# A fused attention, MoE and soft-MoE kernel: F in 512-column matmuls over plain 32x32 transposed tiles, w_out turned in the last pass, b = 7 in program order

## The chip, the cores and the metric

The kernel runs on one core of a Trainium2 chip. The metric is the device time of one execution in microseconds (us). The kernel before takes 537.74 us, the median of three runs (536.98 to 540.11). On this kernel a difference of about 0.5% (2.7 us) is what a measurement can tell from none.

## The reference

An attention between 512 tokens and 32 state rows of each of 8 batches and 8 heads, in both directions, gives 8 x 544 = 4352 rows of 512. These pass a gated two-layer projection and then a soft mixture of experts with 32 slots. Cut to what is computed:

```python
# x (8, 8, 512, 64), state (8, 8, 32, 64)
s = x @ state.T / 8;  xread = softmax(s) @ state        # tokens read the state
s2 = state @ x.T / 8; sread = softmax(s2) @ x           # the state reads tokens
x = concatenate([xread, sread], axis=2)                 # -> (4352, 512)
h = x @ w_in                                            # (512, 2048)
g = where(h >= 1, h, where(h <= -1, 0, (h + 1) ** 2 / 4))
y = g @ w_out                                           # (2048, 512)
logits = y @ phi                                        # 32 slots = 8 experts x 4
d = softmax(logits, over rows);  slot_in = d.T @ y
slot_out = relu(slot_in @ w1[e]) @ w2[e]                # w1 (512, 1024), w2 (1024, 512)
out = softmax(logits, over slots) @ slot_out
```

## The kernel before

y is never formed. With wp = w_out phi the logits are g wp (the matmuls `E`, in `estep`), and slot_in = (d.T g) w_out. So the kernel keeps a running sum over batches of d.T g (`acc`, 32 slots x 2048, laid out over 128 partitions) with a running maximum, and turns it into slot_in once at the end (`SI`).

**Passes.** There is one pass per batch, b = 0 to 7, over its 512 token rows, and a ninth (b = B = 8) over the 256 state rows of all batches (`XS`). A pass has 16 steps m of 128 columns of w_in: `hstep` makes h (12 matmuls of 128x512, each fp32 product from two rounded halves) and g from it (one ScalarE, one GpSimd and one VectorE operation). g lies with its columns on partitions and tokens along the row. Between the steps lie the attention of the next batch (`attention`), the chunks of its x (`vchunk`, matmuls `V`), and, one batch late, the weighting of g.

**F.** d.T g needs g with tokens on partitions. `tstep` turns every 32x32 block of a finished g tile with VectorE and scatters the blocks into one of three places of 4096 columns (`gp0` to `gp2`, each half a batch; `gd_of`) in the order that lets `fall` read 256 columns in a row. `smblock(b)` is a generator of steps that makes the softmax weights (`dRp`, `dR`) and calls `fall`: 128 matmuls of 32x32 weights by 256 columns, in 8 rounds of 16 (half h, row block r), each round filling the 4x4 grid of 32x32 parts of the array (t over array columns, k over array rows); three VectorE operations then fold F into `acc`. Batch 0 goes another way: TensorE turns its g tiles (`tquarter`, tile `gtp`), ScalarE copies them out to `wb`, and four groups of 128x32 matmuls (`F<-wb,dN`, L600 on) and four copies (L605) start `acc`. The ninth pass turns its g the same way into `gp1`, and weights it by the matmuls `P`.

**Weights.** w_in and w_out come as packed words and are converted during batch 0 (`conv_win`, `conv_wo`). For w_out the words go to `acc` one quarter at a time, TensorE turns them (`wtp`, 64 transposes), ScalarE copies them to `wD`, and a DMA writes the turned w_out to DRAM (`wo32`), from where `prefetch` brings it back; `wps`, 4 matmuls for each 2 quarters, makes wp. The end needs 4 MB of w_out, 16 MB of w1 and 16 MB of w2. Their loads are issued in a fixed sequence, one each time a place in SBUF comes free (`give`): six on GpSimd's queue, the others on SyncE's (SP). A load on a queue waits until its place has been read for the last time, and those behind it wait too.

**End.** After the ninth pass: `P`, its transposes `PTp` (L894), `SI` (L901, 16 matmuls of 128x32 by 512), `XDp`, the first expert layer (`h`, L920), `hTp` (L941), and for each half of the 512 columns `SO(0)` and `SO(1)` (L954: w2_0 to w2_7, w2_8 to w2_15), `SR`, the combination of the rows `oV`, `oX`, `oH`, and 16 stores of 512 KB (L993).

**What sets the order.** A list scheduler orders every engine's instructions by readiness and priority, except TensorE's in b = 2 to 6, where the function `steady` runs under a manual schedule and TensorE follows the code. b = 0, 1, 7 and the ninth pass are written in the general loop and ordered by the scheduler on all engines.

Of the kernel before, what the change touches and what calls it, by code (L numbers as in the profile page):

```python
# [16 lines left out]
CFG = dict(wb=12, gv6=(5, 9, 12), lP=((0, 0), (0, 1)), attA=(3, 5, 6, 7, 8, 9, 10, 11), attB=(0, 1, 10, 11, 12), attN=(14, 15), dv=(9, 12, 14), fl=-0.484375, hp=2000, att7=(3, 5, 6, 7, 8, 10), og=1, n3=1, n3m=10, wS=['DP', 'AD', 'AD', 'AD', 'AD', 'DP', 'AD', 'DD', 'AD', 'AD', 'AD', 'AD', 'AD', 'AD', 'AD', 'AD'], xsm=13, k0=5, rg=6, spg=0, att0=6, att=7, V0=(2, 6, 10), Vn=(0, 4, 10), Vx=12, wn='H', wsev='adad', conv=(4, 8, 9, 11, 12, 13, 19, 21, 24, 26, 28, 32, 36, 40, 44, 48, 52, 56, 60), todo=[1, 1, 1, 2, 0, 0, 0, 3, 0, 0, 2, 2, 1, 1, 0, 0], E0=2, E=1, sm=1, tqB=(5, 9, 13), GP=10, pe=(3,), psH=3, gtpX=(0, 7), tq0=(13, 15), keep=(2, 3, 4, 5), x2=(1, 1), natm=1, warm=14, bounce7=(0, 3), split=1, wt=4, so='cscscscscssss', smm=(1, 2, 3, 4, 5, 6, 9), tqv=(), tqvm=0, first='x', apath=2, f32c=1, place=1, attm=(3, 6, 7, 8, 9, 12), subPm=True, loDm=False, bounce=(0, 1, 2, 3), bq=('s', 's'), xq='s', nat=((1, 11), (2, 2), (2, 3), (2, 11), (3, 2), (3, 4), (3, 9), (4, 2), (4, 3), (4, 9), (5, 2), (5, 3), (5, 9), (6, 2), (6, 4), (6, 9)), subP=(1,), mulD=(), loD=(), qlag=0, gv0='EEEEEEEEEEEEEEEE', gv='EEEEEEEEEEEEEEEE', gvS='BBBBBBBBBBBBBBBB')  # L17
# [3 lines left out]
def kernel(  # L21
# [56 lines left out]
    dN = const.tile([128, 4, 32], F32, name="dN")  # L78
# [5 lines left out]
    gp_s = [slot(f"gp{c}", n=4096) for c in range(3)]  # L84
    g0_s = [gp_s[c // 2][:, 2048 * (c % 2):2048 * (c % 2) + 2048] for c in range(6)]
# [48 lines left out]
    cw_w = [acc[:, 512 * i:512 * i + 512] for i in range(4)]  # L134
# [89 lines left out]
    def attention(b):  # L224
# [15 lines left out]

        def over_tokens():
            for G in range(2):
                mx = small.tile([128, 1], F32, tag=f"mx{G}", name="mx")
                nc.vector.tensor_reduce(out=mx, in_=S[G], op=ALU.max, axis=AX.X)
                nb = small.tile([128, 1], F32, tag=f"nb{G}", name="nb")
# [801 lines left out]
```

## Time and profile before

| | |
|---|---|
| median of three runs | 537.74 us |
| runs | 540.11, 536.98, 537.74 us |
| the profiled execution | 533.0 us |
| its span in the profile | 531.0 us (2.0 us lie outside) |
| granted TensorE clock, mean | 0.972 of full |
| first g of b = 0, 1, 2, 3, 4, 5, 6, 7, ninth pass | 33.3, 103.6, 153.7, 201.8, 245.5, 290.0, 334.0, 375.1, 418.7 us |

The rows further down are of this execution. Busy time is counted for each engine by itself, matmuls of different parts of the array run side by side, and "idle before" names the time an engine stood before a group and what released it. The passes b = 2 to 6 take about 44 us each and look alike, so one block, 187 to 231 us, stands for them.

### The profile page before, as it was taken

How to read it: one execution, taken by the hardware profiler on the slowest of the kernel's cores; microseconds unless marked ns; L12 is line 12 of the kernel's file. 1: busy time of each engine (PE TensorE's matmuls, PEld its weight loads, DVE VectorE, ACT ScalarE, POOL GpSimd, SP SyncE). 2: the span in 40 equal slices, each digit the busy share in tenths (PEclk: the TensorE clock that was granted, in tenths of full speed). 3: DMA queues.
4: the chain of work that ended last, by engine and by line, in shares of the span. 5: the costliest groups of instructions: out<-in, count | busy, mean ns of one | idle time of the engine just before them, and what ended most of it. 6: DMA issues, size and time to landing. Idle time of an engine off the chain costs nothing.

```text
span 531.0 us, 12486 instructions
## 1 busy us (share of the span) xinstructions
PE 460.5 (87%) x5262; PEld 276.1 (52%) x5262; DVE 365.1 (69%) x638; ACT 271.9 (51%) x497; POOL 226.4 (43%) x221
## 2 busy tenths in 40 slices
PE   5478697999989999998999999999986989789981
PEld 3135354665546555565655655555653768534550
DVE  2888959566688689689679878967857748315240
ACT  2899767655565365267347536525514436411241
POOL 2443434444465195377348529537515400002220
PEclk9799989999999999999999999999999999999996
DMA  8997727700260130030022013004201679799999
GB/s 312 417 422 330 197 120 160 234 4 3 80 238 1 26 136 0 5 133 27 4 80 80 1 22 141 0 4 153 85 4 41 218 268 386 279 372 423 411 358 299
DMA packets 22551, 85.92 MB, mean 162 GB/s; under 512 B 2017, under 2 KB 10593, under 8 KB 14305
## 3 DMA queue, kind: packets, MB, share of 16 engines
q1 hardware_dynamic: 20976, 77.28, 39.8%
q0 software_dynamic: 1520, 7.87, 4.4%
q8 instruction: 41, 0.67, 0.5%
q14 instruction: 14, 0.11, 0.1%
HBM read 72.03 MB, written 13.11 MB: 160 GB/s over the span
## 4 chain that ended last, share of the span: by engine, by line
PE 42%; DVE 24%; issue 11%; ACT 10%; POOL 6%; DMA 4%; SPq 0%; ACTq 0%; POOLq 0%; DVEq 0%
PE h L437 14%; DVE g L489 5%; DVE gp L512 4%; POOL c L467 4%; PE h L445 3%; PE E L118 3%; PE SO L954 3%; DMA gp<-in_win_dram 3%; PE h L920 3%; POOL a L320 2%; DVE v L387 2%; ACT c L129 2%; PE V L118 2%; PE gtp L507 2%; DVE acc L172 2%
## 5 line engine op out<-in xcount | busy, mean ns | idle before, releaser
L437 PE MATMUL h<-a,v 128*128 128x512 f32 x744 | 196.5, 408 | 12.9 <-DVE g L489 7.3
L467 POOL TENSOR_TENSOR c<-c 128x512 f32<-128x512 f32 x128 | 137.3, 1081 | 149.9 <-ACT c L129 149.3
L437 PEld LDWEIGHTS h<-a,v 128*128 128x128 f32 x744 | 133.6, 189 | 78.6 <-issue 26.6
L129 ACT ACTIVATE c<-h,half 128x512 f32<-128x512 f32 x128 | 86.9, 691 | 96.8 <-PE h L437 46.9
L489 DVE SCALAR_TENSOR_TENSOR g<-h,c 128x512 f32<-128x512 f32 x112 | 75.4, 674 | 38.7 <-POOL c L467 38.5
L512 DVE STREAM_TRANSPOSE gp<-g 128x512 f32<-128x512 f32 x112 | 78.8, 704 | 2.5
L129 ACT ACTIVATE v<-V 128x512 fp32r<-128x512 f32 x62 | 37.2, 600 | 35.8 <-DVE v L387 27.5
L124 PE MATMUL FX<-gp,dR 32*32 32x256 f32 x896 | 38.6, 385 | 2.3 <-issue 2.3
L387 DVE TENSOR_TENSOR v<-V,v 128x512 fp32r<-128x512 f32 x52 | 35.0, 673 | 7.9 <-ACT v L129 7.4
L124 PE MATMUL FV<-gp,dR 32*32 32x256 f32 x882 | 38.2, 385 | 1.3 <-issue 1.3
L124 PE MATMUL V<-win,st_t 64*32 64x512 f32 x448 | 37.0, 623 | 0.0
L118 PE MATMUL V<-win,st_t 64*32 64x512 f32 x64 | 34.7, 623 | 2.3 <-ACT att L129 2.3
L118 PE MATMUL E<-g,wp 128*32 128x512 f32 x56 | 30.0, 619 | 4.6 <-DVE g L489 4.4
L288 POOL TENSOR_TENSOR att<-att,z 128x512 f32<-128x512 f32 x16 | 17.3, 1083 | 31.2 <-DVE rz L252 16.0
L124 PE MATMUL E<-g,wp 128*32 128x512 f32 x168 | 30.4, 619 | 0.0
L445 PE MATMUL h<-XSh,v 128*128 128x256 f32 x128 | 25.0, 288 | 0.9 <-DVE s_gc L493 0.5
L619 DVE SCALAR_TENSOR_TENSOR acc<-acc,al,FV 128x1024 f32<-128x1024 f32 x7 | 9.0, 1281 | 23.4 <-PE FX L124 20.4
L124 PEld LDWEIGHTS FX<-gp,dR 32*32 32x32 f32 x896 | 20.7, 103 | 7.5 <-issue 4.6
L124 PEld LDWEIGHTS FV<-gp,dR 32*32 32x32 f32 x882 | 21.3, 103 | 5.9 <-issue 2.3
L320 POOL TENSOR_TENSOR a<-att,a 128x512 fp32r<-128x512 f32 x14 | 17.8, 1290 | 11.9 <-ACT a L129 11.8
L445 PEld LDWEIGHTS h<-XSh,v 128*128 128x128 f32 x128 | 20.2, 188 | 3.1 <-ACT v L129 0.8
L266 POOL TENSOR_TENSOR att<-att,m 128x512 f32<-128x512 f32 x14 | 15.0, 1081 | 9.4 <-DVE m L265 7.8
(244 smaller groups left out, 765.3 us busy)
## 6 DMA issues: line engine op xcount, KB each, us to landing
w<-in_w_dram SPq DMA_DIRECT2D x23, 1024.0 KB, 9.8
xn<-in_xn_dram SPq DMA_DIRECT2D x8, 1024.0 KB, 6.2
out_dram<-o SPq DMA_DIRECT2D x16, 512.0 KB, 6.7
xs<-in_xs_dram SPq DMA_DIRECT2D x7, 1024.0 KB, 5.0
w<-in_w_dram POOLq DMA_DIRECT2D x6, 1024.0 KB, 5.5
gp<-in_wout_dram SPq DMA_DIRECT2D x5, 1024.0 KB, 11.1
wb<-in_win_dram SPq DMA_DIRECT2D x4, 1024.0 KB, 12.4
wo<-wD SPq DMA_DIRECT2D x16, 256.0 KB, 4.4
```

The source lines that it names most:

```text
L118: first = mm(**calls[0])
L124: e = mm(**c)
L129: return nc.scalar.activation(out=out, in_=in_, func=func, **kw)
L288: (nc.vector if b in CFG["mulD"] else nc.gpsimd).tensor_tensor(out=t3, in0=t3, in1=z1.unsqueeze(2).to_broadcast([128, 16, 32]), op=ALU.mult)
L320: (nc.vector if b in CFG["loD"] or b > 1 and CFG["loDm"] else nc.gpsimd).tensor_tensor(out=lo[:, G, :], in0=raw[G], in1=hi[:, G, :], op=AL ...
L387: nc.vector.tensor_tensor(out=lo[:, G, :], in0=V[G], in1=hi[:, G, :], op=ALU.subtract)
L437: mm(out=h, lhsT=v[:, G, f], rhs=a[:, G, :], start=(k == 0), stop=(k == 5))
L445: mm(out=h, lhsT=w[:, j, :], rhs=x[:, j, :], start=(k == 0), stop=(k == 11))
L467: nc.gpsimd.tensor_tensor(out=c, in0=c, in1=c, op=ALU.mult)
L489: gI[b, m] = nc.vector.scalar_tensor_tensor(out=g, in0=h, scalar=1.0, in1=c, op0=ALU.max, op1=ALU.min)
L512: nc.vector.transpose(out=gd_of(b, m // 8)[:, :, :, m % 8, :].rearrange("p c a i -> p a c i"), in_=gT[b, m].rearrange("p (a c i) -> p a c ...
L920: mm(out=h1[hf][32 * kt:32 * kt + 32, :], lhsT=XD[e // 4][:, kt, 32 * (e % 4):32 * (e % 4) + 32], rhs=w[kt], start=(e == 0), stop=(e == 7))
```

## The change

1. **F.** The three places of 4096 columns become one of 12288, which holds 24 tiles of 512 columns. `tstep` is a plain VectorE transpose of one 128x512 tile into tile ((2b + m // 8) mod 3) x 8 + m mod 8. `fall` reads it with a strided operand (runs of 32 columns, a step of 512 columns from run to run) in 64 matmuls of 32x32 by 512: 4 rounds of 16. `acc` changes its column order, and F is folded in by four VectorE operations of 512 (eight of 256 for b = 1, 4 and 7, whose tiles wrap around the place).
2. **b = 0 by the same way.** `tquarter` is kept for the ninth pass alone; batch 0 gets 16 VectorE transposes in place, four each at (b, m) = (0,11), (0,14), (1,0), (1,2); its E groups stand at (0,10), (0,13), (0,15), (1,1), its `smblock` steps from b = 1, m = 3, and `fall(0)` copies F into `acc`.
3. **w_out.** The words go straight to `wD`, and from there unturned to `wo32`; the 64 transposes and 16 ScalarE copies at the start go. `wturn`, at m = 7 to 14 of the ninth pass, turns the prefetched w_out in place: 8 transposes into one two-bank tile of `psV`, one ScalarE and one VectorE copy, eight times. `SI` has 64 matmuls of 128 columns for its 16 of 512.
4. **b = 7** runs in `steady` too, without attention, with `xsplit` and the first `wsplit` at m = 13.
5. **Places.** All weight loads go to SP's queue. `wb0` and `wb1` are given at b = 1, m = 0 (before: m = 12), `a0` at the start of b = 7. The ninth pass's turned g lies in the two places of `rot_g`, which are given only after `smblock(B)`; the 12288 columns are given in `merge`, behind `fall(7)`, and take w2_10 to w2_15 in six loads in a row (`ends`).

```diff
-    gp_s = [slot(f"gp{c}", n=4096) for c in range(3)]
+    gp = slot("gp", n=12288)
...
+    def gd_of(b, m):
+        n = ((2 * b + m // 8) % 3) * 8 + m % 8
+        return gp[:, 512 * n:512 * n + 512]
...
-        words(i, acc[:, 1024 * h:1024 * h + 1024])
+        words(i, wD[g][:, 2 * h:2 * h + 2, :].rearrange("p k f -> p (k f)"))
         for k in range(2 * h, 2 * h + 2):
-            w = cw_w[k]
-            tp = psX.tile([128, 4, 128], F32, tag="X", name="wtp")
-            for x in range(4):
-                nc.tensor.transpose(tp[:, x, :], w[:, 128 * x:128 * x + 128], ident)
-            act(wD[g][:, :, 128 * k:128 * k + 128], tp)
+            dma(out=wo32[k][:, 512 * g:512 * g + 512], in_=wD[g][:, k])
...
     def tstep(b, m):
-        nc.vector.transpose(
-            out=gd_of(b, m // 8)[:, :, :, m % 8, :].rearrange("p c a i -> p a c i"),
-            in_=gT[b, m].rearrange("p (a c i) -> p a c i", a=4, i=32))
+        nc.vector.transpose(out=gd_of(b, m), in_=gT[b, m])
...
-        for k in range(4):
-            if k >= len(CFG["tq0"]):
-                tquarter(b, k)
-            F = psX.tile([128, 512], F32, tag="X", name="F")
-            group([dict(out=F[32 * t:32 * t + 32, :], lhsT=dN[:, t, :], rhs=nat_of(b, k)[:, t], start=True, stop=True) for t in range(T)])
-            nc.vector.tensor_copy(out=acc_t[:, :, 4 * k:4 * k + 4, :], in_=F.rearrange("p (m k i) -> p k m i", m=4, k=4))
-            yield
...
-        group([dict(out=F[k][32 * t:32 * t + 32, 256 * h:256 * h + 256], lhsT=dR[32 * k:32 * k + 32, r, 32 * t:32 * t + 32],
-                    rhs=gd_of(b, h)[32 * k:32 * k + 32, r, t].rearrange("p m i -> p (m i)"), start=(r == 0), stop=(r == 3))
-               for h in range(2) for r in range(4) for t in range(4) for k in range(4)], chain=True)
-        for a, f in ((acc[:, 0:1024].rearrange("p (k f) -> p k f", k=2), V), (acc[:, 1024:1536], X[0]), (acc[:, 1536:2048], X[1])):
-            nc.vector.scalar_tensor_tensor(out=a, in0=a, scalar=al, in1=f, op0=ALU.mult, op1=ALU.add)
+        u = 2 * b % 3
+        if u < 2:
+            g = gp[:, 4096 * u:4096 * u + 8192].rearrange("p (m t r i) -> p t r m i", t=4, r=4, i=32)
+            halves = [(slice(0, 16), slice(0, 16))]
+        else:
+            g = gp.rearrange("p (u m t r i) -> p t r u m i", u=3, t=4, r=4, i=32)[:, :, :, 0::2]
+            halves = [(slice(0, 8), slice(8, 16)), (slice(8, 16), slice(0, 8))]
+        group([dict(out=F[k][32 * t:32 * t + 32, :], lhsT=dR[32 * k:32 * k + 32, r, 32 * t:32 * t + 32],
+                    rhs=g[32 * k:32 * k + 32, t, r], start=(r == 0), stop=(r == 3))
+               for r in range(4) for t in range(4) for k in range(4)], chain=True)
...
+    def ends():
+        t = slot("ends", tag="gp", n=12288)
+        for j in range(6):
+            i = len(slices) - 6 + j
+            load(i, [t], 2048 * j)
...
+    def wturn(n):
+        k, g = divmod(2 * n, 4)
+        tp = psV.tile([128, 2, 512], F32, tag="V", name="wtp")
+        for j in range(2):
+            w = where["wo", k][1][g + j]
+            for x in range(4):
+                nc.tensor.transpose(tp[:, j, 128 * x:128 * x + 128], w[:, 128 * x:128 * x + 128], ident)
...
-        if 2 <= b <= 6:
+        if 2 <= b < B:
...
-    give("gp1")
+    give([(rot_g, "g", 2048)], [(rot_g, "g", 2048)])
...
-    for i in range(4):
-        for jj in range(4):
-            mm(out=SI[32 * jj:32 * jj + 32, :], lhsT=PT[:, jj, 32 * i:32 * i + 32],
-               rhs=where["wo", i][1][jj], start=(i == 0), stop=(i == 3))
+    group([dict(out=SI[32 * x:32 * x + 32, 128 * k:128 * k + 128], lhsT=PT[:, x, 32 * g:32 * g + 32],
+                rhs=where["wo", k][1][g][:, 128 * x:128 * x + 128], start=(g == 0), stop=(g == 3))
+           for k in range(4) for g in range(4) for x in range(4)], chain=True)
```

The change also packs small tiles in pairs, and adds a function `fine` and some options that nothing uses.

VectorE at the end of batch 0, where the words of w_out's last quarters are made. L157 to L172 (before) and L156 to L171 (after) are these words, `gp` holds g, `v` is a chunk of x. Before:

```order
L387 TENSOR_TENSOR v_115<-V,v_115 128x512 x2
L157 TENSOR_SCALAR acc<-wb_113 128x1024
L159 SCALAR_TENSOR_TENSOR acc<-wb_113,acc 128x1024
L161 SCALAR_TENSOR_TENSOR acc<-wb_113,acc 128x1024
L489 SCALAR_TENSOR_TENSOR gp_109<-h,c 128x512
L170 TENSOR_SCALAR acc<-wb_114 128x1024
```

After:

```order
L428 TENSOR_TENSOR v_113<-V,v_113 128x512
L552 STREAM_TRANSPOSE gp<-gp 128x512 x4
L156 TENSOR_SCALAR wD<-wb_111 128x1024
L169 TENSOR_SCALAR wD<-wb_112 128x1024
L158 SCALAR_TENSOR_TENSOR wD<-wb_111,wD 128x1024
L171 SCALAR_TENSOR_TENSOR wD<-ast,wD 128x1024
L532 SCALAR_TENSOR_TENSOR gp<-h,c 128x512
```

Four transposes of batch 0's second group of g tiles have moved in ahead of the words.

TensorE at the end of b = 7, from the last matmuls of F to the first of the ninth pass (`h<-XSh`). Before:

```order
L437 MATMUL h<-a_749,v_115 128x512 x6
L118 MATMUL V<-win_106,st_t 32x512
L124 MATMUL V<-win_106,st_t 32x512 x7
L118 MATMUL E<-g,wp 32x512
L124 MATMUL E<-g,wp 32x512 x3
L437 MATMUL h<-a_749,v_390 128x512 x18
L118 MATMUL V<-win_107,st_t 32x512
L124 MATMUL V<-win_107,st_t 32x512 x7
L437 MATMUL h<-a_749,v_390 128x512 x6
L437 MATMUL h<-a_749,v_115 128x512 x12
```

After:

```order
L118 MATMUL E<-g,wp 32x512
L124 MATMUL E<-g,wp 32x512 x3
L478 MATMUL h<-a_661,v_382 128x512 x6
L118 MATMUL V<-win_107,st_t 32x512
L124 MATMUL V<-win_107,st_t 32x512 x7
L118 MATMUL E<-g,wp 32x512
L124 MATMUL E<-g,wp 32x512 x3
L478 MATMUL h<-a_661,v_382 128x512 x12
L478 MATMUL h<-a_661,v_113 128x512 x12
```

The E groups and the V chunks have changed their places among the h matmuls of the last steps, and every run of h is 6 or 12 long.

SP's queue in the ninth pass, the loads of w1 and w2 in the order of issue (a w1 or w2 of 128x512 or 128x1024 is a part of one that is spread over several places). Before:

```order
L699 DMA w1_7_4766<-in_w1_dram 128x1024
L699 DMA w1_8_4820<-in_w1_dram 128x2048
L699 DMA w1_11_4843<-in_w1_dram 128x2048 x2
L699 DMA w1_7_4767<-in_w1_dram 128x512
L699 DMA w1_9_4840<-in_w1_dram 128x2048 x2
L699 DMA w1_13_4916<-in_w1_dram 128x2048
```

After:

```order
L738 DMA w1_6_4234<-in_w1_dram 128x2048
L738 DMA ends_4159<-in_w2_dram 128x2048 x6
L738 DMA w1_5_4169<-in_w1_dram 128x512
L738 DMA w1_7_4368<-in_w1_dram 128x2048
L738 DMA w1_4_4166<-in_w1_dram 128x2048
L738 DMA w1_5_4170<-in_w1_dram 128x512
L738 DMA w1_8_4490<-in_w1_dram 128x2048
```

The six loads of `ends` now stand in the queue ahead of w1_7 and all that follow it.

## Rows read from the trace of the kernel before

**Rows 1.** The page, part 1: engine, busy us, share of the span, instructions.

```profile
PE 460.5 (87%) x5262; PEld 276.1 (52%) x5262; DVE 365.1 (69%) x638; ACT 271.9 (51%) x497; POOL 226.4 (43%) x221
```

**Rows 2.** Windows: start:end and length, busy us of each engine, clock, DMA.

```profile
core 0: us, PE busy (x) PEld busy (x) DVE busy (x) ACT busy (x) POOL busy (x), PEclk, DMA share, GB/s
60.00:93.00 33.00, 24.06 (x227) 14.19 (x226) 26.89 (x41) 21.25 (x38) 12.07 (x10) 0.88 0.57 154
93.00:148.00 55.00, 53.54 (x420) 32.81 (x420) 34.84 (x65) 31.92 (x64) 25.12 (x24) 0.98 0.26 87
187.00:231.00 44.00, 41.60 (x548) 24.66 (x548) 35.77 (x64) 22.97 (x45) 25.76 (x25) 1.00 0.14 45
375.00:419.00 44.00, 37.95 (x440) 23.66 (x432) 29.65 (x47) 17.06 (x30) 19.27 (x19) 0.96 0.16 51
434.00:464.00 30.00, 26.35 (x308) 19.86 (x287) 15.85 (x40) 14.00 (x30) 0.52 (x1) 1.00 0.89 334
472.00:488.00 16.00, 15.86 (x144) 6.45 (x144) 7.25 (x11) 2.63 (x6) 4.11 (x3) 1.00 1.01 420
```

**Rows 3.** Timeline of TensorE, a fall and E behind it: start, length, line, operation.

```profile
214.76 0.40 PE L118 MATMUL FV<-gp,dR 32*32 32x256 f32 x1
...
220.64 0.62 PE L118 MATMUL E<-g,wp 128*32 128x512 f32 x1
...
221.09 0.59 PE L118 MATMUL E<-g,wp 128*32 128x512 f32 x1
```

**Rows 4.** Windows of seven falls, instructions on FV alone: sum and mean.

```profile
sum 51.00, PE 38.26 PEld 21.36 DVE 4.78; mean PE 5.47 PEld 3.05 DVE 0.68
```

**Rows 5.** Timeline of VectorE around the same fall.

```profile
220.52 1.28 DVE L619 SCALAR_TENSOR_TENSOR acc<-acc,al,FV 128x1024 f32<-128x1024 f32 x1 [2.96 <-PE FV L124]
221.72 1.40 DVE L619 SCALAR_TENSOR_TENSOR acc<-acc,al,FX 128x512 f32<-128x512 f32 x2
```

**Rows 6.** Groups by line and form, 57 to 154 us: busy us, mean ns.

```profile
L512 DVE STREAM_TRANSPOSE gp<-g 128x512 f32<-128x512 f32 x16 | 11.3, 706 | 0.4
...
L507 PE MATMUL gtp<-cst_t,gp 128*128 128x128 f32 x64 | 9.0, 276 | 0.6 <-ACT att L129 0.4 <-ACT wb L129 0.2
...
L124 PE MATMUL F<-wb,dN 128*32 128x512 f32 x24 | 5.0, 601 | 0.0
...
L605 DVE COPY acc<-F 128x512 f32<-128x512 f32 x4 | 2.7, 677 | 1.7 <-PE F L124 1.7
```

**Rows 7.** Timeline of TensorE, 87 to 100 us.

```profile
90.32 1.06 PE L193 MATMUL wtp<-cst_t,acc 128*128 128x128 f32 x8 [2.08 <-DVE acc L161]
...
94.54 0.87 PE L193 MATMUL wtp<-cst_t,acc 128*128 128x128 f32 x4
...
98.56 0.66 PE L193 MATMUL wtp<-cst_t,acc 128*128 128x128 f32 x4
```

**Rows 8.** Timeline of TensorE, the end of b = 7.

```profile
402.08 1.66 PE L437 MATMUL h<-a,v 128*128 128x512 f32 x6 [1.21 <-DVE g L489]
...
407.96 3.06 PE L437 MATMUL h<-a,v 128*128 128x512 f32 x7 [2.47 <-DVE v L387]
```

**Rows 9.** Timeline of TensorE, the end of the kernel.

```profile
461.90 0.62 PE L118 MATMUL P<-gp,dN 128*32 128x512 f32 x1
...
462.35 0.59 PE L118 MATMUL P<-gp,dN 128*32 128x512 f32 x1
...
466.10 3.64 PE L901 MATMUL SI<-wo,tail 128*32 128x512 f32 x32 [0.75 <-ACT tail L129]
...
488.39 7.11 PE L954 MATMUL SO<-w,hTD 128*32 128x256 f32 x128 [0.52 <-ACT hTD L129]
```

**Rows 10.** Timeline of SyncE's queue: the load behind P, the stores.

```profile
463.92 0.33 SPq L699 DMA_DIRECT2D w<-in_w_dram  x1
...
500.25 24.62 SPq L993 DMA_DIRECT2D out_dram<-o  x16
```

**Rows 11.** The page, part 6: issues, KB each, us to landing.

```profile
out_dram<-o SPq DMA_DIRECT2D x16, 512.0 KB, 6.7
xs<-in_xs_dram SPq DMA_DIRECT2D x7, 1024.0 KB, 5.0
```

More of the change, by code (lines that the diff above doesn't have):

```diff
@@ L83 @@
     win_s = [slot(f"win{c}") for c in range(4)]
[L84 to L85 removed]
+    gp = slot("gp", n=12288)
+    g0_s = [gp[:, 2048 * c:2048 * c + 2048] for c in range(6)]
     xs_s = slot("xs")
@@ L258, in over_slots @@
         def over_slots():
+            m1s = two("m1", 16)
             for G in range(2):
@@ L322, in attention @@
+        if b > 99:
+            yield from fine()
+            return
         apath = b == 0 and CFG["apath"]
@@ L403, in xsplit @@
         act(h, XS)
-        nc.vector.tensor_tensor(out=l, in0=XS, in1=h, op=ALU.subtract)
+        (nc.gpsimd if CFG['xsP'] else nc.vector).tensor_tensor(out=l, in0=XS, in1=h, op=ALU.subtract)
         run["XS"] = h, l
@@ L567, in smblock @@
             run["s"] = small.tile([128, 1], F32, tag="sn", name="sn")
-            nc.vector.tensor_scalar(out=run["s"], in0=bs, scalar1=4.0, scalar2=None, op0=ALU.mult)
+            nc.vector.tensor_copy(out=run["s"], in_=bs)
         else:
@@ L718, in drain @@
             pass
+    def wturn(n):
[5 more added lines that the diff above has]
+                nc.tensor.transpose(tp[:, j, 128 * x:128 * x + 128], w[:, 128 * x:128 * x + 128], ident)
+        for j in range(2):
+            w = where["wo", k][1][g + j]
+            if CFG["wte"][j] == "A":
+                act(w, tp[:, j])
+            else:
+                nc.vector.tensor_copy(out=w, in_=tp[:, j])
     if CFG["first"] == "h":
@@ L761, in steady @@
         nx = None
-        plan = CFG["attB"]
+        plan = CFG["attB"] if A is not None else ()
+        if b == B - 1:
+            give("a0")
         for m in range(NM):
@@ L790, in steady @@
                 step(nx)
+            if b == B - 1 and m == CFG["xsm"]:
+                xsplit()
+            if b == B - 1 and m == CFG["wsm"]:
+                wsplit(0)
         drain(sm)
-        drain(A)
+        if A is not None:
+            drain(A)
         return nx
@@ L799 @@
         last = b == B
-        if 2 <= b <= 6:
-            with tc.manual_schedule(engines={mybir.EngineType.PE}):
+        if 2 <= b < B:
+            with tc.manual_schedule(engines={getattr(mybir.EngineType, e) for e in CFG['eng']}):
                 A = steady(b, A)
@@ L816 @@
                 give("a1")
-                give([(rot_g, "g", 2048)], [(rot_g, "g", 2048)])
             if last:
@@ L833 @@
                     sm = smblock(b - 1)
-            if sm is not None and (m >= CFG["sm"] if b == 1 or last or CFG["smm"] is None else m in CFG["smm"]):
+            if sm is not None and (m >= CFG["sm0"] if b == 1 else m >= CFG["sm"] if last or CFG["smm"] is None else m in CFG["smm"]):
                 step(sm)
@@ L869 @@
                     A = None
-            if last and m == 8:
-                give("gp0", "gp2")
+            if last and m in CFG["wt8"]:
+                wturn(CFG["wt8"].index(m))
             if last and m % 4 == 3:
@@ L879 @@
     estep(B, 3)
-    tquarter(B, 3)
+    tquarter(3)
     sm = smblock(B)
```

172 lines of the change are left out of this document (110 added, 62 removed).

## The prediction

> **What bounds the kernel now.** I read the page's busy shares first, then windows stage by stage, then the timelines of the stages that this change touches. On the page TensorE is busy for 460.5 of 531.0 us [rows 1]. The windows tell where that matters [rows 2]. In a block of the middle passes TensorE works 41.6 of 44 us at full clock and VectorE 35.8: what leaves TensorE there shortens the block, as long as VectorE does not grow past it. From 93 to 148 us, when batch 0's g is turned and weighted, TensorE works 53.5 of 55 us and VectorE 34.8, so TensorE bounds that stage still more plainly. From 60 to 93 us TensorE works only 24.1 of 33 and waits, among others, for the words of w_out [rows 7]: nobody's share is full, a chain of conversions sets the time. The stage of b = 7 has 6.05 us of idle TensorE in 44 and a clock of 0.96. From 472 us on the DMA engines are at share 1.01 with 420 GB/s [rows 2], and the stores end the kernel [rows 10].
>
> **F, passes 1 to 6.** A fall starts at 214.76 and the E behind it at 220.64 [rows 3], so it takes 5.88 us; the busy time of its half on FV is 5.47 on the mean of seven [rows 4]. Two passes of E over 512 columns start 0.45 us apart (220.64 and 221.09) [rows 3]; half of that, 0.225, is what 256 columns cost at the same rate. A fall is 8 rounds of 2 passes, 16 x 0.225 = 3.6 us of streaming; the other 2.28 us lie around the rounds, 0.285 each. After the change it is 4 rounds of 2 passes of 0.45, again 3.6, and 4 x 0.285 = 1.14: 4.74 us, **1.14 less**. The bounds: 0.24 less if most of the overhead goes with the column count, 2.3 less if none of it is left. I take the middle, since the weights to be loaded for a round are the same 16, and their number of rounds halves. VectorE has 2.96 us of idle time ahead of the fold [rows 5], and its fold goes from 2.68 us (1.28 and 1.40 [rows 5]) to 4 x 0.70 = 2.8 us, or for b = 4 and 7 eight halves of perhaps 0.45, 3.6. That is up to 0.9 us on an engine with 8 us to spare per block, so I cost it at nothing; were that cover gone it would be 0.9 us in two blocks. The transposes have the same size, so they stay at 706 ns [rows 6]. Six falls (b = 1 to 6) lie ahead of the ninth pass: 6 x 1.14 = **6.9 us less** (bounds 1.4 and 13.8).
>
> The Trainium skill, "TensorE: Matmul & The Clock Gate", section "Measured speedup vs the span model", puts a pack of 16 tiles at one matmul's length and 15 times about 4 ns. By it a round's overhead is an estimated 0.06 us, and halving the rounds saves 0.24 us of a fall, 1.4 of six; the sum below would come out 5.5 us later. The row speaks against it so far, with 0.285 us around each round, but no row shows what of that a longer round keeps; this is rival 2.
>
> **The start, 93 to 148 us.** What TensorE loses: the 64 transposes `gtp`, 9.0 us, and the groups `F<-wb,dN`, 5.0 us [rows 6]; the last transposes of w_out, 0.87 + 0.66 = 1.5 us [rows 7]; three of four E groups of batch 0, 3 x 0.9 = 2.7 us by two passes of 0.45 each [rows 3], which now stand before b = 1 where TensorE idles. What it gains: fall(0), 4.74 us, and four transposes for dR, 4 x 0.14 = 0.6. So 53.5 - 18.2 + 5.3 = 40.6 us. VectorE gains 8 of the 16 transposes (the others lie ahead of 93 us), 8 x 0.706 = 5.6 us, and trades four copies of 0.677 [rows 6] for the same: 34.8 + 5.6 = 40.4 us. Both are now alike. If TensorE still set the stage, at the middle block's share of 41.6 / 44, it would be 43 us, 12 less; if VectorE did, at its share there of 35.8 / 44, 50 us, 5 less. I take 46, **9 us less**, between the ends since each will sometimes wait for the other; for the range I keep 0 (rival 1) and 12. Ahead of 93 us I take no gain although the 48 transposes left there and their ScalarE copies go: in VectorE's order four of the transposes of batch 0 now stand in front of the words of w_out's last quarters, 4 x 0.706 = 2.8 us, and TensorE waits for just these words (2.08 us [rows 7]); the two about cancel, with 4 us either way.
>
> **b = 7.** Its waits are TensorE's own order: 1.21, then 2.47 us behind operations that VectorE finishes late [rows 8]. In the order of the code the h matmuls stand in runs of 6 and 12 with V and E between, as in the middle blocks. There 2.4 us idle remain in 44, here 6.05: 3.65 us less, and at full clock its 37.95 us of work shrink by 4%, 1.5 us [rows 2]. Together **5 us less** (bounds 0 and 7). The engine's order holds also for the head of the ninth pass, where nothing else is queued to fill a wait; that is in the lower bound.
>
> **The ninth pass and the end.** `wturn` adds 64 transposes on TensorE. Eight take 1.06 us [rows 7], so 8.5 us, in a stage where it is the bound: from 434 to 464 us it is busy for 26.35 of 30 [rows 2]. I take 1.6 us of it as filling idle time, and fall(7) gives 1.14 back: P comes 5.8 us later. `SI` in 64 matmuls of a quarter of the columns costs about the 3.64 us of before [rows 9]; I add 0.4. So the expert layers come 6.2 us later on TensorE alone, and SO(0), which ended at 488.39 + 7.11 = 495.5 [rows 9], would end at 501.7.
>
> The loads are later still. Before, `gp1` came free with P, at 463.92 [rows 10]. Now the places of `rot_g` come free there, at 463.9 + 5.8 = 469.7, and 13 loads of 1 MB in SP's order run from there to w2_7, the last that SO(0) needs. The first lands 5.0 us later [rows 11], the others follow at 1.05 MB / 420 GB/s = 2.5 us each [rows 2]: 469.7 + 5.0 + 12 x 2.5 = 504.7, and the last eighth of SO(0) ends 0.9 later, at 505.6, 10.1 us later than before. The chain from there to the end had a slack of about 2.5 us before, since w2_15 was the 16th load behind P (463.9 + 5.0 + 15 x 2.5 = 506.4) and SO(1) waited for it; now w2_10 to w2_15 are there early, by `ends`. So the end comes **7.5 us later**. The DMA side agrees: the last two loads land at 509.7, 3.3 us later than before, and the stores took 24.6 us from first to last issue [rows 10], so the stores alone would give 3.3. Bounds: 1 us (the turns fill idle time, places come earlier) and 12 (the six loads of `ends` also hold up w1_7 and those behind them, which the first expert layer waits for).
>
> **The sum** against the profiled execution: -6.9 - 9 - 5 + 7.5 = -13.4, 531.0 to 517.6 of span, 533.0 to 519.6 in all. The median of the runs is 4.7 above the profiled execution, so the median should go to 537.74 - 13.4 = **524.3 us**.
>
> **Rivals.**
>
> 1. VectorE becomes the bound of the start. For it: its 40.4 us against TensorE's 40.6, and the words of w_out behind the transposes. Then 93 to 148 us gains about 1.5 and not 9: 524.3 + 7.5 = 531.8.
> 2. A round's overhead goes with its columns, so that 512 columns cost nearly twice a round of 256. Falls gain 0.24 and not 1.14 each, fall(0) is 5.6: 524.3 + 5.5 + 0.9 + 0.9 = 531.6. Against it: the weights per round are the same.
> 3. Slower than before: the strided operand of `fall`, each run of 32 columns 2 KB from the next, is read at half the rate. A fall is then 8 passes of 0.9 and 1.14, 8.3 us: 2.4 more and not 1.14 less for each of the six and for fall(7), and 3.6 more for fall(0), so 7 x 3.6 + 3.6 = 28.8 above the forecast: 553. It decides once the other terms, -9 - 5 + 8.6 = -5.4, are used up: by eight falls at 0.7 more than before each, a pass of about 0.67. Against it: P reads runs of 32 with a step of 128 columns, and its passes start at 461.90 and 462.35 [rows 9], 0.45 apart as E's do; a step of 512 is not shown.
> 4. Nothing is gained in sum: the start gains 4, b = 7 gains 2, the falls 3.5, and the end loses 9.5, the transfers of w1 and w2 being what the late places delay: 537.7.
>
> **How the numbers follow.** The forecast has a chance of 0.52, with a range of its own of 516 to 531; rival 1 has 0.17, rival 2 0.13, rival 3 0.08, rival 4 0.10. 512 to 534 leaves out rival 3, most of rival 4 and a little of the forecast's low end. A measurement of this kernel can tell 0.5% (2.7 us) from no change. Faster by more (below 535.0): forecast, rivals 1 and 2, and a part of rival 4, 0.84. Within 0.5%: most of rival 4, 0.07. Slower: rival 3 and what is left, 0.09.
>
> **What would show it.** In the trace after, the fall of a middle block from its first matmul to the E behind it: 4.7 us (rival 2: 5.6; rival 3: over 8). Passes of 0.45 in it. The distance from the first g of b = 1 to that of b = 2, 50.1 us before: about 9 shorter, with TensorE's share below 0.95 there; if VectorE's is above it, rival 1. b = 7's 44 us window at clock 1.00 with some 2.4 us idle. In the end, SO(0) waiting for w2 around 500 us, P 5 to 6 us later against the ninth pass's first g, stores that start later but run without loads beside them. I am wrong if the h of the first expert layer waits for w1, if the ninth pass grows by more than 8 us, or if the middle blocks keep 44 us although the falls got shorter, VectorE then being what a block waits for.

## The result and the profile after

The changed kernel takes 514.36 us, the median of four runs (512.69 to 517.83), beside 537.82 us for the kernel before; the ratio is 0.961, with an interval of 0.953 to 0.969. Timed once more beside the last runs below it is 513.64 us (513.21 to 515.45) and 0.961 (0.957 to 0.965). The forecast was 524.3 us in a range of 512 to 534: the sign and the range held, but the gain is 23.5 us where 13.4 were forecast.

The page after, parts 1 and 4 (answers to [rows 1]), and behind them part 4 of the page before:

```profile
span 513.6 us, 10998 instructions
PE 449.2 (87%) x4497; PEld 262.5 (51%) x4497; DVE 378.6 (74%) x681; ACT 261.6 (51%) x473; POOL 221.1 (43%) x214
PE 42%; DVE 31%; DMA 10%; ACT 7%; POOL 5%; issue 2%; SPq 0%; ACTq 0%; DVEq 0%; POOLq 0%
PE 42%; DVE 24%; issue 11%; ACT 10%; POOL 6%; DMA 4%; SPq 0%; ACTq 0%; POOLq 0%; DVEq 0%
```

TensorE has 765 instructions less and 11 us less work, VectorE 13.5 us more, and the DMA engines now hold 10% of the chain that ended last, for 4%: something at the end waits for a transfer. The windows after, start:end and length, then busy us of each engine, granted clock and DMA (answers to [rows 2]; the second is the stretch of the start that the prediction spoke of, the fourth b = 7, the fifth the ninth pass, the last the wait of SO(0)):

```profile
core 0: us, PE busy (x) PEld busy (x) DVE busy (x) ACT busy (x) POOL busy (x), PEclk, DMA share, GB/s
60.00:90.00 30.00, 23.74 (x190) 12.91 (x198) 26.11 (x43) 16.24 (x29) 11.81 (x10) 0.77 0.38 133
90.00:142.00 52.00, 47.83 (x467) 25.73 (x452) 42.52 (x82) 26.44 (x52) 27.95 (x26) 1.00 0.33 122
190.00:233.00 43.00, 40.70 (x422) 23.31 (x421) 35.98 (x67) 23.20 (x45) 25.54 (x25) 1.00 0.15 50
356.00:391.00 35.00, 32.98 (x307) 19.29 (x292) 28.64 (x44) 15.74 (x29) 15.67 (x15) 1.00 0.07 24
391.00:441.00 50.00, 48.77 (x514) 39.47 (x513) 34.90 (x82) 27.85 (x59) 3.18 (x4) 1.00 0.79 307
464.00:479.00 15.00, 9.43 (x129) 4.56 (x130) 0.56 (x1) 0.77 (x2) 0.00 (x0) 0.89 1.01 415
```

Where the time went, by marks that both traces have (first g of a pass; first matmul of the ninth pass; `PTp`; the end of the span). Of each difference the part that the shorter falls explain stands beside it, measured from the first matmul of a fall to the first matmul of something else:

| stretch | before | after | difference | of it falls | forecast, with falls |
|---|---|---|---|---|---|
| start to first g of b = 3 | 201.8 | 190.0 | -11.8 | -1.8 | -10.1 |
| first g of b = 3 to that of b = 7 | 173.3 | 165.8 | -7.5 | -6.0 | -4.6 |
| b = 7, to the first `h<-XSh` | 40.5 | 34.9 | -5.6 | -1.0 | -6.1 |
| ninth pass, to `PTp` | 49.1 | 50.1 | +0.9 | -2.4 | +5.8 |
| `PTp` to the end | 66.3 | 72.8 | +6.5 | | +1.7 |
| span | 531.0 | 513.6 | -17.4 | | -13.4 |

The first g of b = 0, 1, 2 and 3 after come at 33.1, 99.8, 147.2 and 190.0 us. The two profiled executions differ by 17.4 us, the medians by 23.5; the other 6 us are taken up below, with the executions' clock.

The start up to the first g of b = 3, once more as windows: before, after, and after without batch 0's transposes (a run further down):

```profile
33.30:201.80 168.50, 148.64 (x1365) 87.96 (x1365) 128.17 (x215) 106.96 (x195) 82.35 (x74) 0.97 0.40 137
33.10:190.00 156.90, 138.22 (x1211) 75.14 (x1208) 134.78 (x236) 92.61 (x163) 81.86 (x74) 0.95 0.40 147
33.50:180.60 147.10, 135.26 (x1259) 73.06 (x1248) 123.76 (x219) 91.83 (x163) 83.21 (x74) 0.98 0.42 156
```

TensorE has 10.4 us less to do there, VectorE 6.6 us more, and TensorE stands idle for 18.7 us, where it was 19.9.

The timeline of TensorE, one fall of the middle passes after (answers to [rows 3]; start, length, line, operation):

```profile
202.94 0.61 PE L118 MATMUL FV<-gp,dR 32*32 32x512 f32 x1
203.40 0.59 PE L118 MATMUL FV<-gp,dR 32*32 32x512 f32 x1
```

The two passes of a round start 0.46 us apart, as those of E over 512 contiguous columns did: the strided operand is read at the full rate. All falls but the first take 4.39 us, 4 rounds of 0.90 and 0.20 around each. Before, that of [rows 3] took 5.88 us, 8 rounds of 0.45 and 0.285; the seven on FV and FX took 5.4 to 6.8. The fold on VectorE behind it (answers to [rows 5]):

```profile
207.41 1.41 DVE L661 SCALAR_TENSOR_TENSOR acc<-acc,al,FV 128x512 f32<-128x512 f32 x2 [1.66 <-PE FX L124]
208.74 1.40 DVE L661 SCALAR_TENSOR_TENSOR acc<-acc,al,FX 128x512 f32<-128x512 f32 x2
```

It takes 2.8 us as costed, and VectorE still waits for the fall ahead of it.

TensorE around `P`, two lines of before and then after (answers to [rows 9]):

```profile
461.31 0.27 PE L588 MATMUL dNp<-cst_t,dT 64*128 64x64 f32 x1 [0.74 <-ACT dT L129]
464.69 0.65 PE L894 MATMUL PTp<-cst_t,tail 128*128 128x128 f32 x4 [0.87 <-DVE tail L598]
...
436.01 1.09 PE L783 MATMUL wtp<-cst_t,wo 128*128 128x128 f32 x8
437.04 0.27 PE L626 MATMUL dNp<-cst_t,dT 64*128 64x64 f32 x1
...
437.91 1.92 PE L632 MATMUL P<-natS,dN 128*32 128x512 f32 x16 [0.43 <-ACT dN L129]
439.76 1.09 PE L783 MATMUL wtp<-cst_t,wo 128*128 128x128 f32 x8
440.73 0.66 PE L973 MATMUL PTp<-cst_t,tail 128*128 128x128 f32 x4
```

Two of the eight groups of w_out's turns lie where TensorE waited for ScalarE and VectorE before, 0.74 us ahead of `dNp` and 0.87 ahead of `PTp`. TensorE at the two `SR` before, then in SO(0) and at the two `SR` after:

```profile
496.06 0.70 PE L961 MATMUL SR<-tail,cst_t 128*128 128x256 f32 x2 [0.56 <-ACT tail L129]
...
510.78 0.70 PE L961 MATMUL SR<-tail,cst_t 128*128 128x256 f32 x2 [0.50 <-ACT tail L129]
...
464.49 1.93 PE L1032 MATMUL SO<-w,hTD 128*32 128x256 f32 x32 [0.52 <-ACT hTD L129]
470.07 6.14 PE L1032 MATMUL SO<-w,hTD 128*32 128x256 f32 x80 [3.65 <-DMA w<-in_w_dram]
477.08 1.07 PE L1032 MATMUL SO<-w,hTD 128*32 128x256 f32 x16 [0.86 <-DMA w<-in_w_dram]
478.71 0.70 PE L1039 MATMUL SR<-tail,cst_t 128*128 128x256 f32 x2 [0.56 <-ACT tail L129]
...
493.42 0.70 PE L1039 MATMUL SR<-tail,cst_t 128*128 128x256 f32 x2 [0.50 <-ACT tail L129]
```

SO(0) waits for w2 twice, 4.5 us in sum. From one `SR` to the other it is 14.71 us, for 14.72 before.

### The profile page after: what moved, and what is told of

It reads as the page before. It is cut to its first block, busy times and chain, and to the rows that moved or that the text cites. A ratio compares the mean times of both kernels' runs of the same rounds, so it can differ in the third digit from the quotient of the medians.

```text
span 513.6 us, 10998 instructions
## 1 busy us (share of the span) xinstructions
PE 449.2 (87%) x4497; PEld 262.5 (51%) x4497; DVE 378.6 (74%) x681; ACT 261.6 (51%) x473; POOL 221.1 (43%) x214
## 4 chain that ended last, share of the span: by engine, by line
PE 42%; DVE 31%; DMA 10%; ACT 7%; POOL 5%; issue 2%; SPq 0%; ACTq 0%; DVEq 0%; POOLq 0%
PE h L478 15%; DVE gp L552 7%; DVE g L532 6%; DMA w<-in_w_dram 6%; PE h L486 4%; PE FV L124 3%; PE E L118 3%; DMA gp<-in_win_dram 3%; POOL a L316 3%; DVE v L428 3%; PE FX L124 2%; POOL c L508 2%; PE V L118 2%; PE SO L1032 2%; PE wtp L783 1%
## 5 line engine op out<-in xcount | busy, mean ns | idle before, releaser
L478 PE MATMUL h<-a,v 128*128 128x512 f32 x744 | 200.4, 414 | 17.7 <-DVE g L532 9.0
L478 PEld LDWEIGHTS h<-a,v 128*128 128x128 f32 x744 | 135.2, 192 | 87.1 <-issue 28.2
L428 DVE TENSOR_TENSOR v<-V,v 128x512 fp32r<-128x512 f32 x52 | 34.9, 672 | 2.0 <-ACT v L129 1.3
L124 PE MATMUL FX<-gp,dR 32*32 32x512 f32 x512 | 35.7, 598 | 0.0
L124 PE MATMUL FV<-gp,dR 32*32 32x512 f32 x496 | 35.4, 597 | 0.0
L118 PE MATMUL E<-g,wp 128*32 128x512 f32 x56 | 29.2, 604 | 4.3 <-DVE g L532 4.0
L124 PE MATMUL E<-g,wp 128*32 128x512 f32 x168 | 29.6, 605 | 0.0
L1067 DVE COPY o<-oV 128x512 f32<-128x512 f32 x6 | 4.2, 692 | 25.6 <-PE oX L124 25.6
L661 DVE SCALAR_TENSOR_TENSOR acc<-acc,al,FV 128x256 f32<-128x256 f32 (+1 forms) x20 | 10.6, 584 | 14.5 <-PE FX L124 14.5
L1075 POOL DMA_DIRECT2D out_dram<-o x16 | 8.0, 507 | 30.3 <-DVE o L1067 30.3
L124 PEld LDWEIGHTS FV<-gp,dR 32*32 32x32 f32 x496 | 14.7, 103 | 9.6 <-issue 6.8
```

Source lines behind the costliest of these rows:

```text
L118: first = mm(**calls[0])
L124: e = mm(**c)
L428: nc.vector.tensor_tensor(out=lo[:, G, :], in0=V[G], in1=hi[:, G, :], op=ALU.subtract)
L478: mm(out=h, lhsT=v[:, G, f], rhs=a[:, G, :], start=(k == 0), stop=(k == 5))
L661: nc.vector.scalar_tensor_tensor(out=a, in0=a, scalar=al, in1=f, op0=ALU.mult, op1=ALU.add)
```

## The experiments

**The kernel before, again.**

> The kernel before, unchanged, once more. It is there for a second trace: the profiled execution of before took 533.0 us, 4.7 below its median, so the difference of the two traces (17.4 us of span) is 6 us short of the difference of the medians (23.5). Theory A: one execution of before differs from another by a few us at one place (a stage in which TensorE waits and the clock drops), and a second trace shows a span of 534 to 538 with one stage longer by 3 to 6 us. Rival: the second trace has the same 531 us and the same stages, and the medians are raised by something outside the span. Time: no change.

It took 536.11 us (ten runs), ratio 1.002 (0.998 to 1.007). Its trace has a span of 531.2 us and, from the first g of b = 1 on, every mark within 0.7 us of the first trace, so the traces don't show what its longer executions lose: the profiled ones, 533.0 and 533.2 us, both lie at the low end of the spread. Theory A's stage was not found. What the runs do show is the mean clock. In the last comparison below, eleven executions of before fall in two groups: 531.4 to 532.8 us at 0.968 to 0.972 (four), 535.1 to 537.7 us at 0.956 to 0.966 (seven). The order isn't strict: of the ten here, those of 532.7 and 533.2 us are at 0.961 and one of 536.0 us at 0.966.

**Rounds of the fall.** The matmuls of a fall are cut in two, on the new layout:

```diff
-    rhs=g[32 * k:32 * k + 32, t, r], start=(r == 0), stop=(r == 3))
-   for r in range(4) for t in range(4) for k in range(4)], chain=True)
+    rhs=part(h, k, t, r), start=(r == 0), stop=(r == 3))     # 256 columns
+   for h in range(2) for r in range(4) for t in range(4) for k in range(4)], chain=True)
```

> The changed kernel with the falls alone cut back: each matmul of 512 columns in two of 256, 8 rounds of 16 for 4, on the new layout with its strided operand. Theory: the rounds are what the falls gained by, so each of the eight falls goes from 4.39 back to about 5.9 us, TensorE is the bound in all of these passes, and the kernel is 8 x 1.5 = 12 us slower, about 526. Rival 1: the gain comes from elsewhere (the layout, the order of weights): falls stay at 4.4 to 4.7 us and the time at 514. Rival 2: falls are 5.9 but VectorE or GpSimd fills the blocks now, so that only half of it, 5 to 7 us, is seen.

532.26 us, ratio 0.993 (0.989 to 0.997): 18 us slower than the changed kernel. Windows of one of its falls, instructions on FV alone:

```profile
206.00:213.50 7.50, 5.84 (x128) 3.26 (x128) 0.69 (x2) 1.00 0.02 4
```

Its eight falls take 5.2 to 7.7 us, 50.3 together, where the changed kernel's take 35.2: 15.1 of the 17.2 us by which the spans differ; another 2.8 us lie between the two `SR` (17.48 us), where the clock was 0.81. So the number of rounds, with the matmuls and weight loads that double with it, is what the falls gained by, and TensorE pays for it about one to one. Rival 1 and rival 2 of this run fall. The first and the last fall are the longest with 256 columns (7.5 and 7.7 us); why those two was not tried.

**b = 7 in the general loop.** One line is undone:

```diff
-        if 2 <= b < B:
+        if 2 <= b <= 6:
```

> The changed kernel with b = 7 back in the general loop, where the scheduler orders TensorE. Theory: the order is worth what the traces show from the first g of b = 7 to the first matmul of the ninth pass, 5.6 us less of which 1.0 is the fall: 4.6 us slower, about 519. Rival: with the other parts in place the scheduler's order is as good, and less than 1.5 us is lost.

528.05 us, ratio 0.982 (0.974 to 0.989): some 11 us slower by the ratios, where 4.6 were expected. TensorE at the end of its b = 7 (timeline), and windows of b = 7 and of the stretch behind SO(0):

```profile
381.08 1.66 PE L478 MATMUL h<-a,v 128*128 128x512 f32 x6 [1.21 <-DVE g L532]
...
386.97 3.36 PE L478 MATMUL h<-a,v 128*128 128x512 f32 x7 [2.47 <-DVE v L428]
```

```profile
354.00:394.00 40.00, 34.40 (x291) 19.91 (x290) 28.20 (x44) 15.63 (x27) 16.30 (x15) 0.96 0.06 22
482.00:508.00 26.00, 24.84 (x199) 13.01 (x199) 5.67 (x9) 5.76 (x12) 4.10 (x8) 0.67 0.55 186
```

The two waits of [rows 8] are back to the digit, 1.21 and 2.47 us, and b = 7 takes 40.3 us for 34.9: 5.4 us. The start was 1.9 us quicker in this execution. The other 11.0 us of the 14.5 of span lie between the two `SR` (25.71 us for 14.71), where TensorE ran for a good part at its lower level (0.67 on the mean over 26 us), with the same instructions as the changed kernel, which kept 1.00 there. SO(0) waits 4.7 us for w2 in it and 4.5 in the changed kernel.

**The same with another order of w2.** The place of 24 tiles takes w2_0 to w2_5 in this kernel and in the next:

```diff
-            i = len(slices) - 6 + j
+            i = 20 + j
```

> b = 7 back in the general loop, and w2_0 to w2_5 in the place of 24 tiles, both at once. With b = 7 in the loop alone the kernel lost 11 to 14 us, of which only 3.5 stand before the ninth pass; the rest lies behind SO(0)'s wait for w2, where its clock was 0.67 over 26 us against 1.00. Theory: the wait is what drops the clock there, by chance of its place; without the wait the tail runs at full clock and the loss is 3.5 to 5 us against the kernel with the w2 order alone, 513.5 to 515. Rival: the order of b = 7 costs the tail in another way (places that come later), and the loss stays at 11 us or more, 521.

515.07 us, ratio 0.964 (0.959 to 0.969). Against the kernel with the w2 order alone (507.3 to 510.0 us, below) that is 5 to 8 us slower; in the traces (the second one of that kernel) all of it, 6.6 us, stands before the ninth pass, and from there to the end they take 116.4 and 116.5 us. With the wait of SO(0) gone, the loss of clock behind it is gone too. That fits the theory, and so do the other traces: of the seven in which SO(0) waits for w2, three have the lower level between the two `SR` (17.48, 17.48 and 25.71 us from one to the other); of the five with the other order of w2 none has (14.71 or 14.72). It isn't a proof, since four have the wait and no such loss, the changed kernel's two among them.

**w2_0 to w2_5 first.**

> The changed kernel, but the six loads into the place of 24 tiles fetch w2_0 to w2_5 and not w2_10 to w2_15, so that the first half of the second expert layer finds them there and the late places get w2_6 to w2_15. Theory: the end of the changed kernel is set by SO(0), which waits 5.0 us for w2 (its 128 matmuls take 13.7 us for 7.1 before) and pushes everything behind it; with w2_7 landing about 15 us earlier the wait goes, and with it 6 to 6.5 us of the whole, to about 508 us. Rival: the DMA engines are the bound of the end, the loads land at 482 us in either order and the stores follow them; then nothing is gained (514 us), or SO(1) waits for w2_15 in place of SO(0).

> The changed kernel with w2_0 to w2_5 in the place of 24 tiles, timed again. Theory: without the wait of SO(0) it is 4 to 7 us below the changed kernel on the same chip, 508 to 510. Rival: 2 us or less, the rest of the 6.5 us of wait being given back in SO(0) itself, which took 9.4 us for 7.7 at a clock of 0.83 in the first trace.

509.97 us, ratio 0.948 (0.942 to 0.954), and on the chip of the last comparison 507.26 us, 0.950 (0.946 to 0.954), 6.4 us below the changed kernel's 513.64 there. TensorE in SO(0) of that second run:

```profile
462.67 5.39 PE L1032 MATMUL SO<-ends,hTD 128*32 128x256 f32 x96 [0.52 <-ACT hTD L129]
467.88 1.91 PE L1032 MATMUL SO<-w,hTD 128*32 128x256 f32 x32
470.35 0.70 PE L1039 MATMUL SR<-tail,cst_t 128*128 128x256 f32 x2 [0.56 <-ACT tail L129]
```

SO(0) no longer waits, and `SR` comes 7.7 us behind its start for 14.2. The DMA engines are as full as before, but nothing that lands last is needed first, and the rival falls. This version beats both kernels. Its first trace had SO(0) at a clock of 0.83 and 1.7 us longer (9.37 us from its start to `SR`); its second had 1.00 and 7.68.

**Without the turns of w_out.**

> The changed kernel without the turns of w_out in the ninth pass (64 transposes and 16 copies are left out, w_out goes unturned into SI, which is a part of the computation left undone). It prices the turns. The prediction had 8.5 us of transposes, 1.6 of it in idle time: 6.9 us. Theory now: they cost about 5 us, since in the trace 7 groups of eight stand 0.8 to 0.9 us apart from the next matmul, one lies in the wait ahead of P and one in that ahead of PTp; so P and everything behind it come 5 us earlier, and the kernel is about 509. Rival A: the idle time of the ninth pass takes them all and nothing moves (514). Rival B: the full 8.5 us (506).

511.09 us, ratio 0.956 (0.951 to 0.961), some 2.6 us by the ratios. The trace is sharper, since the ninth pass starts at a different time in each execution: from its first matmul to `PTp` it is 46.8 us without the turns and 50.1 with them, so 64 transposes, with the 16 copies behind them, cost **3.2 us**. This stretch in windows, with the turns and without:

```profile
390.68:440.73 50.05, 48.82 (x514) 39.51 (x513) 34.90 (x82) 27.86 (x58) 3.50 (x4) 1.00 0.78 305
389.10:435.92 46.82, 42.77 (x451) 32.62 (x449) 30.34 (x75) 24.50 (x51) 3.50 (x4) 1.00 0.80 313
```

The turns add 6.05 us of work, and 2.8 of it lie in idle time, which goes from 4.05 us to 1.23. The timeline without them, ahead of `PTp`:

```profile
432.51 0.27 PE L626 MATMUL dNp<-cst_t,dT 64*128 64x64 f32 x1 [0.74 <-ACT dT L129]
...
435.92 0.66 PE L971 MATMUL PTp<-cst_t,tail 128*128 128x128 f32 x4 [0.90 <-DVE tail L635]
```

The waits that the turns had filled stand open again. With 46.8 us and no turns the pass is 2.3 us shorter than before's 49.1, which is what its fall gained.

**Batch 0's transposes behind the words of w_out.** One dependency in VectorE's order:

```diff
+                    if (b, m) == (0, 14):
+                        tc.add_manual_dep(e.ins, gI[0, 14].ins.name, ORDER, reason="behind")
```

It was suggested by the changed kernel's timeline of VectorE and TensorE:

```profile
74.56 2.49 DVE L552 STREAM_TRANSPOSE gp<-gp 128x512 f32<-128x512 f32 x4 [2.51 <-PE E L124]
76.98 0.65 DVE L156 TENSOR_SCALAR wD<-wb 128x1024 uint32<-128x1024 uint32 x1
...
82.13 0.68 DVE L532 SCALAR_TENSOR_TENSOR gp<-h,c 128x512 f32<-128x512 f32 x1
...
82.86 2.93 PE L478 MATMUL h<-a,v 128*128 128x512 f32 x6 [4.15 <-DVE gp L532]
```

> The changed kernel with one order added on VectorE: the four transposes of batch 0's second group stand behind the g of its step 14, no longer ahead of the words of w_out at 74.6 us. Theory: these four (2.5 us) and four word operations (5.1 us) hold up the g of step 12, TensorE waits 4.15 us for it, and its clock falls (0.77 from 60 to 90 us); moved away, the wait shrinks by 2.5 us or more and the first g of b = 1 comes 2 to 4 us earlier, to about 511. Rival: the words alone hold up g (they come first then) and VectorE, which works 35.6 of 42 us from 100 to 142, is late by the same 2.5 us afterwards; nothing is gained, 514.

> Both improvements together: the four transposes behind step 14, and w2_0 to w2_5 first. Theory: they lie in different stages and add, 7 us for the w2 order and 2 to 4 for the transposes: about 504. Rival: what the start gains, the loads or the first half of the second expert layer take back (the tail of the kernel with the w2 order alone still has a DMA share of 1.01 to 1.04): 508.

> The same with the four transposes of batch 0 behind the g of step 14, timed again. In the traces the first g of b = 1 came 6.3 us earlier by this, that of b = 2 3.5, that of b = 3 2.1 to 2.7. Theory: 2 to 3 us below the kernel with the w2 order alone. Rival: within 1 us of it, the rest being inside of what executions differ by.

Alone 515.12 us, ratio 0.964 (0.959 to 0.970); with the w2 order 508.36 us, 0.951 (0.947 to 0.956), and once more 508.69 us, 0.952 (0.948 to 0.956), where the w2 order alone has 507.26. No gain. In the traces the first g of b = 1 comes 4 to 6 us earlier, that of b = 2 between 3.5 earlier and 0.3 later: what the earlier words give is in part lost again in b = 1. The rival's time held; that VectorE is what takes it back is not shown. The trace of the run alone was still 1.9 to 2.7 us ahead at the first matmul of the ninth pass, and lost 2.8 us between the two `SR` at a clock of 0.81.

**Without batch 0's transposes.**

> The changed kernel without the 16 VectorE transposes of batch 0 (left undone, so that F of batch 0 is made from unturned tiles). It prices them: 10 us of VectorE between 74 and 105 us. Theory, as the prediction had it: TensorE and VectorE are near their limits alike in the start, so a part of it, 4 to 6 us by the first g of b = 2, and as much of the whole, 509. Rival 1 of the prediction (VectorE bounds the start): 8 to 10 us, 505. Rival, TensorE bounds it: 2 us or less, 513.

509.73 us, ratio 0.954 (0.949 to 0.958), against 513.64 us of the changed kernel, repeated beside it:

> The changed kernel once more, beside the two kernels with another w2 order on the same chip. Expected 512 to 516 us, 0.957 to 0.964 of the kernel before. Between executions I expect the time to follow the mean granted clock, as in the runs so far (512.7 us at 0.970, 517.8 at 0.950). Rival: the executions scatter without regard to the clock.

The first g of b = 2 comes at 137.1 us for 146.2 and 147.2 in the two traces of the changed kernel: 9 to 10 us for 16 transposes that take 10 to 11. The window of the start without them:

```profile
60.00:90.00 30.00, 27.21 (x228) 14.17 (x229) 24.02 (x41) 19.16 (x36) 15.52 (x12) 0.90 0.55 199
```

TensorE works 27.2 of 30 us there, at a clock of 0.90, for 23.7 at 0.77 in the changed kernel. So in the start these transposes are paid nearly one to one: up to the first g of b = 3 TensorE stands idle for 11.8 us without them, for 18.7 with them. Of the 9 to 10 us the whole kept about 4 by the medians, 6 by the spans. In the trace they are there up to the first `SR` (469.02 us for 478.71 and 477.87), and 3.2 us go between the two `SR`, 17.94 us for 14.71 at a clock of 1.00. The scheduler has put the same matmuls there in another order, with two groups of `oX` alone, at 478.10 and 481.77 us, that stand beside `oV` or `oH` in the changed kernel. The first:

```profile
478.10 1.13 PE L124 MATMUL oX<-tail,LT 32*128 32x256 f32 x4
```

So the time of the whole run does not price the transposes; the marks of the start do.

In the repeated runs the changed kernel scatters little (513.2 to 513.7 us at a clock of 0.964 to 0.968, then 514.6 and 515.5 at 0.962), and the time again goes with the clock, if roughly; the run without batch 0's transposes has 508.9 us at 0.965 and 510.0 at 0.972.

## Why the prediction was right, and where its sizes were off

**Falls.** The mechanism held, and e2's 256 columns show it. The size was low: 1.14 us of gain per fall was forecast from overhead that halves with the rounds (0.285 us each), measured were 1.0 to 1.8, on the mean of the six 1.48, since the overhead of a round also fell to 0.20. Six falls gave 8.9 us for 6.9. Rival 2 wanted 5.6 us a fall and rival 3 over 8, and 4.39 rules both out; against rival 3 the passes of [rows 9] on P spoke for a full rate, and 0.46 us confirm it for a step of 512. The Trainium skill, "TensorE: Matmul & The Clock Gate", section "Measured speedup vs the span model", whose 15 times about 4 ns for one pack make an estimated 0.06 us a round, does not agree with the traces of rounds one behind the other: they have 0.20 to 0.285 us around each round of 16 fp32 matmuls, and the measurement decides. Its section "The mechanism" says that a weight load overlaps a running matmul only where its row group differs. That would explain a price per round, as all four row groups are in use in one; no run here separates the loads from the rest.

**The start.** Forecast 9 us less, measured 10.0 up to the first g of b = 3 without the fall. The sum was right, its place was not, and that is luck. All 9 were to lie between 93 and 148 us and none ahead. The prediction's own mark, from the first g of b = 1 to that of b = 2, went from 50.1 to 47.4 us, 2.7 less (48.8 in the second trace) and not 9. Of the rest 3.8 came ahead of the first g of b = 1 (6.2 in the second trace), where the prediction had let the gain and the four transposes cancel, and 3.5 in the pass b = 2 besides its fall. In part that is work that moved: before, 80 matmuls of `V` lie between the first g of b = 2 and that of b = 3 and 48 in the pass ahead, after it is 64 in each. What the start gained is what TensorE lost in work, 10.4 us of the 11.6 between the first two windows of the start above; no run puts batch 0's old way or the turns of w_out back, so which of them gave how much stays open. The run without batch 0's transposes shows that VectorE holds TensorE up in the start now, as rival 1 said. By the shares that were named as its sign it did not come: from the first g of b = 1 to that of b = 2 TensorE is busy for 0.91 and VectorE for 0.86. Its error was its price, since VectorE could hold TensorE up and the start still gain 10 us in all. The prediction's other remark, four transposes in front of the words, was right in place: TensorE waits 4.15 us for the g behind them and its clock drops (0.77 from 60 to 90 us); but moving them gained nothing.

**b = 7.** Forecast 5 us less, measured 4.6 without the fall, and 5.4 to 6.9 when it is undone. The waits named, 1.21 and 2.47 us, are the ones that come back.

**The ninth pass.** This step failed. 64 transposes were priced at 8.5 us by 8 in 1.06, with 1.6 us of idle time filled; they cost 3.2. Most of the error is the length: 1.06 us runs from a group's first start to its last end, but in this pass the next matmul mostly starts 0.8 to 0.9 us behind a group's start, and all 64 add 6.05 us to TensorE's work, 2.4 less than priced. The rest is the gaps: 2.8 us of the transposes filled idle time, 1.2 more than allowed. The turns have nobody waiting for them until `SI`, so the scheduler could lay some where TensorE stood, and the pass before had 3.65 us of idle TensorE between 434 and 464 us [rows 2], of which I took less than half. With the fall's 2.4 us the pass grew by 0.9 for the 5.8 forecast.

**The end.** This step failed the other way: +6.5 us from `PTp` for +1.7. The loads did come as worked out: w2_7 landed 37 us behind `P`, for 35 forecast, and SO(0) waited. What was wrong is the slack of 2.5 us behind it, that SO(1) had waited for w2_15 before. It had not: its last 64 matmuls begin 10.56 us behind the first `SR` before and 10.55 after, where their w2 landed long ahead. From the first `SR` to the second it was 14.72 us before and 14.71 after, a chain of TensorE with ScalarE and VectorE between, with no wait for a load, and from the second to the end 20.20 and 20.14; so what delayed SO(0) delayed the end in full. The two errors, 4.9 us too much and 4.8 too little, cancel in the sum by luck, and the order of w2 shows that the second was a matter of six indices.

**From the trace to the median.** The forecast carried the 4.7 us between before's profiled execution and its median over to the kernel after. That was the term behind the remaining 6 us: before's profiled execution lies 4.8 below its median, the changed kernel's 1.0 above. Before has executions at 531 to 533 us and more at 535 to 538, on the whole the longer the lower their mean clock, and both its traces are of executions at 533; the changed kernel's executions lie at 513 to 515.5 on the same chip. That the clock is the cause is argued from this, not shown, and which stage of before would lose it stays open: no trace of before shows an execution above 533.2 us.

So of the 10 us between forecast and result, about 2 are the falls, 1 the start, 1.5 the middle passes (the stretch to b = 7 gained that much beyond its falls; b = 7 itself 0.4 less than forecast), and 6 what executions differ by. Why a middle pass gained 0.4 us beyond its fall is not shown. The ninth pass and the end are right only together, and the start only as a whole.

## What to carry to other kernels

Work that has no early consumer should be priced by what it adds to the engine's busy time, from a group's start to the start of what follows, and not by its length from start to end; then list the waits of the stage and charge only what doesn't fit into them. Before granting slack behind a late transfer, take two marks behind it and see whether the chain between them waits at all; if it doesn't, order the transfers by first use. A forecast for the median from one profiled execution needs the executions' own spread, and which end of it the profile shows.

## What was not expected of the hardware

The same instructions at the same place ran at either level of TensorE's clock in different executions. Of one kernel, that with w2_0 to w2_5 first, SO(0) took 9.37 us at a clock of 0.83 in one trace and 7.68 in the other. Of two kernels, the stretch between the two `SR` ran at 1.00 in the changed kernel and at 0.67 over 26 us with b = 7 in the loop, behind waits of SO(0) of 4.5 and 4.7 us. It cost 11 us of one trace, more than the change of order that the run was made for. And the matmuls of 32x32 by 512 carry less around each round than those by 256, 0.20 us for 0.285, though the same 16 weights are loaded; a fall of them took 4.38 to 4.46 us in every trace, where those by 256 took 5.2 to 7.7.
